# Fills in one shared score bank, VectorE tiles in the third banks, an earlier last output product, and Q ahead of K in an attention-and-gated-MLP kernel

## The chip, the cores and the metric

One core of a Trainium2 chip. The metric is the device time of one execution in microseconds (us). All runs used here are of the fast state; most executions of a kernel agree within half a per cent (61 of the 64 of the kernel before are within 0.5% of their common median). "Span" is the time from the first to the last instruction of the profiled execution; it is about 2 us shorter than the device time of the same execution (736.1 of 737.96 for the kernel before). The experiments ran in three later calls, on three chips. The kernel before ran in each of them, with medians of 739.65, 739.92 and 738.97 us, so kernels of different calls are compared by their ratios to before rather than by their medians.

## The reference

```python
x: (1, 2048, 512) bf16                  # 2048 tokens
q, k, v = (x @ wqkv) -> 32 heads of 16
o = softmax(q @ k.T / 4) @ v            # 32 x 2048 x 2048 scores
a = o @ wo
b = ((x @ w_gate) * (x @ w_up)) @ w_down    # inner width 1376
g = sigmoid((x * gate_w).sum(-1))
out = g * a + (1 - g) * b
```

## The kernel before

The exponential is the big item: the 32 x 2048 x 2048 scores are 2048 tiles of 128 keys (partitions) by 512 queries. A tile goes one of two ways. **ScalarE tiles** (1536 at first) take a table exponential, two or three tiles in one instruction. **VectorE tiles** (512 at first) take an integer trick on VectorE plus three shifted copies, shared by VectorE and GpSimd. TensorE makes scores, the products with V, and all "fills": the Q, K, V, gate, up, down and output products.

The kernel divides PSUM into eight banks of 128 x 512 fp32: slots A and B of three banks each (`psS`, 128 x 3072), one bank X (`psX`) and one for the sums over V (`psO`). ScalarE reads the first two or three banks of the slots in turn. Five more words: a **cell** is a place in SBUF for one tile of exponentials (in `PT`, or in `wv`, `hT` or `wd` while these are not needed for their own data); it is free again when its product with V is done. A **quad** is four heads, a **head block** eight, a **chunk** 512 queries. A **pack** is four 32-wide matmuls that run side by side (in the trace of before the four start within about 0.01 us of each other, and packs of 512 columns that follow each other directly 0.215 to 0.228 us apart). The normalised output of a quad goes to `OT`, for every second quad by way of `OX` and four DMAs.

The kernel is a **planner**: while it is built, it plays the five engines forward with assumed durations and fixes each engine's instruction order. Each engine then runs in that order and waits on semaphores. `st["ua"]` counts ScalarE tiles issued so far; every fill has a position `pos` in that count.

```python
# a score group: which third bank goes to what (cut)
use3 = "a"                                   # three ScalarE tiles
if late > (FA1 if b else FA0): use3 = "f"    # a late fill takes the third bank
elif lag >= (LA1 if b else LA0): use3 = "d"  # a VectorE tile takes it
if dleft and lag > LC: convert()             # VectorE too far behind: give a tile to ScalarE
...
# where a fill may start (cut)
if st["ua"] < 96 or late > FA1: cand.append(slots[1][2])
if st["ua"] < 96 or late > FA0: cand.append(slots[0][2])
if st["ua"] < 96 or not can or late > XF or not d_pick(...): cand.append(X)
...
FA0 = 20; FA1 = 0; LA0 = 2; LA1 = 0; XF = 24; LC = 3
```

The tail of before: when all scores are done, four banks take the output product of the last chunk over all but the last quad (`tail_first`, 16 packs); then the last quad is normalised in four pieces, its packs are added, and four combines (`ost`, two buffers) go out by DMA.

## Time and profile before

| | before |
|---|---|
| device time, median | 739.64 us (740.08 with the run beside the changed kernel) |
| profiled span | 736.1 us |
| ScalarE busy | 709.0 us, 96% |
| TensorE busy | 695.5 us, 94% |
| first exponential / end of the last | 10.1 / 723.4 us |

The profile's first part gives each engine's busy time, then the span in 40 slices with the busy share in tenths, then the chain that ended last. A row of groups reads: line, engine, operation, output<-input with shapes, count | busy us, mean ns | idle before, and what ended it. The lines themselves are shown in the prediction. I split the time with the start of each exponential in the trace: time to the first; **floor** = 0.904 us for each two-tile instruction, 1.331 for each three-tile one, the durations from start to start when nothing is in the way, and 0.478 for a single tile (worked out from these two; no kernel has more than two); **stalls** = the rest up to the end of the last exponential; **tail**.

### The profile page before, as it was taken

The numbers are of one execution on the slowest core, as the hardware profiler recorded it, in microseconds if no ns is written. First come the engines' busy times: TensorE is split into PE (matmuls) and PEld (weight loads), VectorE is DVE, ScalarE is ACT, GpSimd is POOL, SyncE is SP. The second block draws the span as 40 slices with busy tenths as digits, with TensorE's granted clock in tenths as the row PEclk, the third lists the DMA queues.
The fourth block names the chain that finished last, engine by engine and source line by source line (L and its number), as shares of the span: only waits on it lengthen the run. The fifth ranks groups of instructions, "written<-read, shape, count | busy, mean of one in ns | idle before, by whom it ended". The sixth has DMA issues, their size and how long they took to land.

```text
span 736.1 us, 21656 instructions
## 1 busy us (share of the span) xinstructions
PE 695.5 (94%) x9177; PEld 204.7 (28%) x9177; DVE 636.2 (86%) x1179; ACT 709.0 (96%) x703; POOL 409.6 (56%) x432
## 2 busy tenths in 40 slices
PE   8999999999999999999989999999999899899897
PEld 3323333322222222222222222222222222222222
DVE  5888978798898999989979988889889789998785
ACT  5999999899999999999999999999999899999994
POOL 3756885154656556566775654466566454655341
PEclk9999999999999999999999999999999999999999
DMA  7700000002000010000000100000000100000000
GB/s 143 243 4 17 20 17 18 17 4 97 18 19 19 13 32 24 20 17 17 20 8 21 38 27 17 17 12 12 20 17 19 32 18 20 16 21 17 17 19 31
DMA packets 31015, 21.66 MB, mean 29 GB/s; under 512 B 18344, under 2 KB 25928, under 8 KB 30920
## 3 DMA queue, kind: packets, MB, share of 16 engines
q1 hardware_dynamic: 29048, 19.49, 8.9%
q8 instruction: 73, 1.20, 0.7%
q10 hardware_dynamic: 1872, 0.79, 0.5%
q14 instruction: 22, 0.18, 0.1%
HBM read 15.11 MB, written 2.35 MB: 24 GB/s over the span
## 4 chain that ended last, share of the span: by engine, by line
ACT 64%; PE 8%; DVE 1%; DMA 1%; issue 0%; SPq 0%; POOL 0%; DVEq 0%
ACT PT L1545 52%; ACT wv L1545 13%; PE psO L1081 3%; PE psS L502 2%; PE psS L900 1%; PE psX L900 1%; PE psS L1092 1%; DVE PT L958 1%; DVE PT L1014 0%; DMA OT<-OX 0%; SPq L1166 0%; DMA out_dram<-ost 0%; DVE ost L793 0%; POOL OX L1153 0%; DVE usb L701 0%
## 5 line engine op out<-in xcount | busy, mean ns | idle before, releaser
L1545 ACT ACTIVATE PT<-psS 128x1024 bf16<-128x1024 f32 (+1 forms) x509 | 556.7, 1278 | 6.8 <-PE psO L1081 4.4
L1017 POOL TENSOR_SCALAR PT<-PT 128x1024 int16<-128x1024 int16 x325 | 336.3, 1046 | 259.7 <-DVE PT L1014 153.7
L900 PE MATMUL psS<-QM,KE 32*128 32x512 bf16 x1731 | 270.2, 385 | 10.6 <-ACT PT L1545 5.0
L958 DVE TENSOR_SCALAR PT<-psX 128x512 int16<-128x512 f32 x313 | 214.3, 685 | 42.3 <-PE psS L900 36.1
L1081 PE MATMUL psO<-PT,VS 128*18 128x512 bf16 x1656 | 222.2, 381 | 1.0 <-POOL PT L1017 0.4
L1081 PE MATMUL psO<-PT,VD 128*18 128x512 bf16 x1428 | 210.2, 382 | 1.9 <-POOL PT L1017 1.2
L1014 DVE TENSOR_SCALAR PT<-PT 128x1024 int16<-128x1024 int16 x382 | 169.4, 481 | 4.6 <-PE psO L1081 1.7
L1545 ACT ACTIVATE wv<-psS 128x1024 bf16<-128x1024 f32 (+1 forms) x122 | 142.1, 1204 | 0.3
L900 PE MATMUL psX<-QM,KE 32*128 32x512 bf16 x317 | 120.4, 380 | 15.0 <-ACT PT L1545 5.5
L958 DVE TENSOR_SCALAR PT<-psS 128x512 int16<-128x512 f32 x183 | 123.8, 684 | 12.2 <-PE psS L900 10.9
L900 PEld LDWEIGHTS psS<-QM,KE 32*128 32x128 bf16 x1731 | 68.5, 91 | 165.3 <-ACT PT L1545 67.5
L900 PEld LDWEIGHTS psX<-QM,KE 32*128 32x128 bf16 x317 | 28.7, 90 | 144.1 <-issue 44.5
L1081 PE MATMUL psO<-wv,VS 128*18 128x512 bf16 x256 | 65.4, 382 | 0.6 <-POOL PT L1017 0.3
L1081 PEld LDWEIGHTS psO<-PT,VS 128*18 128x18 bf16 x1656 | 52.1, 88 | 44.1 <-issue 29.9
L1081 PEld LDWEIGHTS psO<-PT,VD 128*18 128x18 bf16 x1428 | 49.2, 88 | 44.2 <-issue 24.9
L502 PE MATMUL psS<-wd,hT 128*32 128x512 bf16 (+1 forms) x704 | 53.2, 384 | 1.0 <-ACT PT L1545 0.9
L502 PE MATMUL psS<-xT,wu 128*32 128x512 bf16 x656 | 53.4, 384 | 0.4 <-DVE QM L557 0.2
L502 PE MATMUL psS<-xT,wg 128*32 128x512 bf16 x640 | 49.4, 383 | 0.2 <-DVE usb L701 0.2
L1545 ACT ACTIVATE hT<-psS 128x1024 bf16<-128x1024 f32 (+1 forms) x39 | 40.5, 1114 | 6.1 <-PE psS L900 6.0
L701 DVE CAST usb<-psS 128x512 bf16<-128x512 f32 (+1 forms) x42 | 28.6, 681 | 4.5 <-PE psS L502 4.3
L733 DVE TENSOR_TENSOR hT<-psS,usb 128x512 bf16<-128x512 f32 (+1 forms) x41 | 27.9, 681 | 2.9 <-PE psS L502 2.2
L1153 POOL TENSOR_TENSOR OX<-oraw,rb 128x512 bf16<-128x512 f32 x15 | 19.1, 1273 | 12.9 <-DVE PT L1014 7.9
(97 smaller groups left out, 471.1 us busy)
## 6 DMA issues: line engine op xcount, KB each, us to landing
rb<-rscr SPq DMA_DIRECT2D x31, 256.0 KB
out_dram<-ost SPq DMA_DIRECT2D x16, 128.0 KB, 1.7
wu<-in_B_w_up_dram SPq DMA_DIRECT2D x1, 1376.0 KB, 10.2
wg<-in_B_w_gate_dram SPq DMA_DIRECT2D x1, 1376.0 KB, 12.7
wd<-in_B_w_down_dram SPq DMA_DIRECT2D x1, 1280.0 KB, 6.1
OT<-OX SPq DMA_DIRECT2D x60, 16.0 KB, 1.8
wo<-in_A_wo_dram SPq DMA_DIRECT2D x1, 512.0 KB, 10.6
den<-oraw SPq DMA_DIRECT2D x31, 8.0 KB
```

What stands on the lines that cost most here:

```text
L502: return e.matmul(out_ap[32 * q : 32 * q + w, :], lhs[:, 32 * q : 32 * q + w], rhs, start=s0, stop=s1, tile_position=(0, 32 * q), skip_gro ...
L701: lambda v: v.tensor_copy(usb[0:w, n % 2, :], bk.ap[0:w, :]),
L733: lambda v: v.tensor_tensor(hT[0:w, f, :], bk.ap[0:w, :], usb[0:w, n % 2, :], ALU.mult),
L900: r = e.matmul(bk.ap, KE[32 * j : 32 * j + 32, b, kt * 128 : (kt + 1) * 128], QM[32 * j : 32 * j + 32, p, b, :], start=True, stop=True, ti ...
L958: lambda v: v.tensor_scalar(cell_ap(pr["cell"] + i, 1, mybir.dt.int16), bk.ap, CB, 0.0, ALU.add, ALU.max),
L1014: fn = lambda v: v.tensor_single_scalar(cell_ap(c, n, I16), cell_ap(pr["cell"], n, I16), 32.0 * k, ALU.add)
L1017: fn = lambda g: g.tensor_scalar(cell_ap(c, n, I16), cell_ap(pr["cell"], n, I16), 32.0 * k, 1.0, ALU.add, ALU.mult)
L1081: r = e.matmul(psO[32 * j : 32 * j + VW, :], pv_stationary(m, kt, j, k), cell_ap(cell, 1), start=s0, stop=s1, tile_position=(0, 32 * j), s ...
L1092: r = e.matmul(DB.ap[32 * j : 32 * j + 32, :], ones[:, k, :], cell_ap(cell, 1), start=s0, stop=s1, tile_position=(0, 32 * j), skip_group_c ...
L1153: lambda e: e.tensor_tensor(dst, oraw[:, s, :], rb[:, s, :], ALU.mult),
L1545: lambda a: a.activation(cell_ap(c, n), src, ACT.Exp, scale=LN2 / 128.0),
```

## The change

The intent is to keep fills out of the slots, so that score groups do not wait for a fill's eviction; to drive ScalarE with the measured overhead; and to take work from both ends.

```diff
-        FA0 = 20          # fills may take third banks when late
-        FA1 = 0
-        LA0 = 2
-        LA1 = 0
-        XF = 24
+        FA0 = 99          # practically never
+        FA1 = 99
+        LA0 = 0           # VectorE tiles take third banks readily
+        LA1 = 1
+        XF = -99          # X is always open to fills
-        LC = 3            # conversion limit
+        LC = 6
-        LAP = 0.0
+        LAP = 0.1
-                0.065 + 0.4267 * n,     # assumed exponential time, n tiles
+                0.052 + 0.4267 * n,
-                        lat=2.2,        # OT<-OX transfer
+                        lat=3.2,
-        ED = 330
+        ED = 380
-        F0 = 190.0; WP = 40.0; F1 = 1500.0
+        F0 = 210.0; WP = 36.0; WL = 18.0; F1 = 1490.0
... (start)
-        for f, bk in ((f_k(0, 0, 0), slots[0][2]), (f_q(0, 0, 0), slots[1][2])):
+        for f, bk in ((f_q(0, 0, 0), slots[1][2]), (f_k(0, 0, 0), slots[0][2])):
+                if b == ch == 0:        # first K evicted by ScalarE
+                    ev_k[b, ch] = add("act", [last], lambda a: a.activation(dst, bk.ap, ACT.Copy), ...)
-            if can and t + PACK > max(tE, tL) + 0.08:
+            if ua == 0 or (can and t + PACK > max(tE, tL) + 0.08):   # no fill before the first scores
... (tail)
-            for tt in range(4 if c < NCH - 1 else 0):
-                fills.append(f_wo(c, tt, ...))
+            for tt in range(4):        # the last chunk's product too, as fills at NA - WL
+                fills.append(f_wo(c, tt, ... if c < NCH - 1 else NA - WL))
-        def tail_first(t, force=False): ...    (removed)
+        # combine() of these writes fp32 partial sums, o_dst = part[:, tt, :];
+        # the final combine adds the last quad to them, into four buffers wk[:, tt, :]
```

(Cut: the same assumed time in two more places, two bookkeeping lines, the loop's end condition.)

More of the change, by code (lines that the diff above doesn't have):

```diff
@@ L527, in evac @@
                 bk.need += 1
+                dst = KE[:, b, ch * 512 : (ch + 1) * 512]
+                if b == ch == 0:
+                    ev_k[b, ch] = add(
+                        "act", [last], lambda a: a.activation(dst, bk.ap, ACT.Copy), 0.48, lat=0.66, cb=lambda k: bk.readers.append(k)
+                    )
+                    return
                 ev_k[b, ch] = add(
@@ L530, in evac @@
                     [last],
-                    lambda v: v.tensor_copy(KE[:, b, ch * 512 : (ch + 1) * 512], bk.ap),
+                    lambda v: v.tensor_copy(dst, bk.ap),
                     0.61,
@@ L786, in _build @@
         otfree = {}
+        ev_part = {}
+        part = xT[:, :, 512:1536].bitcast(F32)
         def combine(t, bank_ap, last, cb=None, halves=None):
             c, tt = divmod(t, 4)
+            fin = t >= T - 4 and halves is None
+            o_dst = ost[:, t % 2, :] if t < T - 4 else part[:, tt, :] if not fin else wk[:, tt, :]
+            src = part[:, tt, :] if fin else b_ap(t)
             k = add(
                 "dve",
-                [last, ev_b[c, tt], ogate["g"], o_out.get(t - 2)],
-                lambda v: v.scalar_tensor_tensor(
-                    ost[:, t % 2, :], bank_ap, gval[:, t : t + 1], b_ap(t), ALU.mult, ALU.add
-                ),
+                [last, ev_b[c, tt], ogate["g"]] + ([o_out.get(t - 2)] if t < T - 4 else [ev_part[tt]] if fin else [pe["last"]]),
+                lambda v: v.scalar_tensor_tensor(o_dst, bank_ap, gval[:, t : t + 1], src, ALU.mult, ALU.add),
                 0.67,
@@ L799, in combine @@
             )
+            if t >= T - 4 and not fin:
+                ev_part[tt] = k
+                return
             bfree[t] = k
@@ L803, in combine @@
                 [k],
-                lambda e: e.dma_start(out2[t * 128 : (t + 1) * 128, :], ost[:, t % 2, :]),
+                lambda e: e.dma_start(out2[t * 128 : (t + 1) * 128, :], o_dst),
                 0.1,
@@ L812, in f_wo @@
             t = 4 * c + tt
+            lastc = c == NCH - 1
             packs = [
                 (
-                    lambda bk, b=b: col(bk.ap, OT[:, (NB * c + b) % NOT, tt * 128 : (tt + 1) * 128], wo[:, b, :], b == 0, b == NB - 1),
+                    lambda bk, b=b: col(
+                        bk.ap,
+                        OT[:, (NB * c + b) % NOT, tt * 128 : (tt + 1) * 128],
+                        woz[:, 0, :] if lastc and b == NB - 1 else wo[:, b, :],
+                        b == 0,
+                        b == NB - 1,
+                    ),
                     PACK,
@@ L825, in evac @@
                 bk.need += 1
-                combine(t, bk.ap, last, cb=lambda k: bk.readers.append(k))
+                combine(t, bk.ap, last, cb=lambda k: bk.readers.append(k), halves=True if lastc else None)
             def deps():
+                if lastc:
+                    if any(f.name[0] in "ugkvq" for f in fills):
+                        return [None]
+                    return [d_wo, d_woz[0], ev_b.get((c, tt)), o_mult.get(NM - 2)] + [o_ot.get(NB * c + b) for b in range(NB - 1)]
                 if t >= 2 and t - 2 not in o_out:
@@ L1194, in _build @@
         GP = 200.0
-        F0 = 190.0
-        WP = 40.0
-        F1 = 1500.0
+        F0 = 210.0
+        WP = 36.0
+        WL = 18.0
+        F1 = 1490.0
         fills.append(f_gate(GP))
@@ L1212, in _build @@
                 fills.append({"u": f_u, "g": f_g, "d": f_d}[kind](c, i, pos))
-            for tt in range(4 if c < NCH - 1 else 0):
-                fills.append(f_wo(c, tt, max(PER * NQ * (c + 1) + WP, f0 + step * (c + 1) + 4.0) + 9.0 * tt))
+            for tt in range(4):
+                fills.append(f_wo(c, tt, max(PER * NQ * (c + 1) + WP, f0 + step * (c + 1) + 4.0) + 9.0 * tt if c < NCH - 1 else NA - WL))
         for c in range(NCH - 1):
@@ L1270, in do_fill @@
                 f.bank.need -= 1
-                FE.append((f, f.bank, f.t0, k))
                 f.evac(f.bank, k)
+                FE.append((f, f.bank, f.t0, k, qs["dve"][-1] if qs["dve"] else None))
                 if f.name[0] == "v":
@@ L1281, in act_need @@
             for a in exps:
-                tt += 0.065 + 0.4267 * len(a[0])
+                tt += 0.052 + 0.4267 * len(a[0])
             return tt
@@ L1436, in pe_step @@
                     return True
-            if can and t + PACK > max(tE, tL) + 0.08:
+            if ua == 0 or (can and t + PACK > max(tE, tL) + 0.08):
                 return False
-            if not aleft and not dleft and (pv_ready(t) is None) and tail_first(t):
-                return True
             if dleft and lag_() > LDO:
@@ L1457, in _build @@
         tailb = []
-        def tail_first(t, force=False):
-            c = NCH - 1
-            tt = len(tailb)
-            if tt == 4:
-                return False
-            deps = [d_wo, d_woz[0]] + [o_ot.get(NB * c + b) for b in range(NB - 1)] + [o_mult.get(NM - 2)]
-            for bk in (X, slots[1][2], slots[1][0], slots[0][0], slots[1][1], slots[0][1]):
-                if bk in tailb or bk.free_at() is None or not (force or bank_free(bk, t)):
-                    continue
-                if not force and any(d is None or d.end is None or d.end + SEM > t for d in deps):
-                    return False
-                deps += bk.take(99)
-                tailb.append(bk)
-                cs = slice(tt * 128, (tt + 1) * 128)
-                def fn(e):
-                    r = None
-                    for b in range(NB):
-                        r = col(bk.ap, OT[:, (NB * c + b) % NOT, cs], wo[:, b, :] if b < NB - 1 else woz[:, 0, :], b == 0, False)(e)
-                    return r
-                pe_run(deps, fn, 4 * PACK, "c", t)
-                return True
-            return False
         def filler(t, can=True):
@@ L1545, in act_step @@
                 lambda a: a.activation(cell_ap(c, n), src, ACT.Exp, scale=LN2 / 128.0),
-                0.065 + 0.4267 * n,
-                lat=0.065 + 0.4267 * n + 0.21,
+                0.052 + 0.4267 * n,
+                lat=0.052 + 0.4267 * n + 0.21,
             )
@@ L1666, in _build @@
         o_xt[0] = o_xt[-KD]
-        for f, bk in ((f_k(0, 0, 0), slots[0][2]), (f_q(0, 0, 0), slots[1][2])):
+        for f, bk in ((f_q(0, 0, 0), slots[1][2]), (f_k(0, 0, 0), slots[0][2])):
             fills.append(f)
             start_fill(f, bk)
-            if f.name == "k00":
-                f.deps = lambda: [d_wk[0]]
+            if f.name == "q00":
+                f.deps = lambda: [d_wq[0]]
                 f.pdeps = [[o_xt[-1 - kt]] for kt in range(KD)]
@@ L1681, in _build @@
                 clock[e] += 0.02
-            if pvst["m"] >= NM:
+            if pvst["m"] >= NM and not fills and st["fill"] is None:
                 break
@@ L1696, in _build @@
         assert not fills and st["fill"] is None, [f.name for f in fills]
-        while len(tailb) < 4:
-            assert tail_first(clock["pe"], True)
         c = NCH - 1
+        tailb = [X, slots[1][2], slots[1][0], slots[0][0]]
         lastpv = pvst["last"]
@@ L1726, in _build @@
                 pe_run(
-                    [mt],
-                    col(tailb[tt].ap, OX[:, (NB - 1) % 2, cs], woz[:, 1, :], False, True),
+                    [mt] + tailb[tt].take(99),
+                    col(tailb[tt].ap, OX[:, (NB - 1) % 2, cs], woz[:, 1, :], True, True),
                     PACK,
```

## The prediction

> **What bounds the kernel now.** I read the busy table and the 40 slices first, to see which engine is full and when.
>
> ```profile
> PE 695.5 (94%) x9177; PEld 204.7 (28%) x9177; DVE 636.2 (86%) x1179; ACT 709.0 (96%) x703; POOL 409.6 (56%) x432
> ...
> ACT  5999999899999999999999999999999899999994
> ...
> ACT 64%; PE 8%; DVE 1%; DMA 1%; issue 0%; SPq 0%; POOL 0%; DVEq 0%
> ```
>
> ScalarE is full in every slice but the first and last, and the chain that ended last lies on it for 64% of the span. TensorE is close behind. So time can come from four places only: what ACT does before its first exponential, the length of its exponentials, its stalls between them, and what follows the last one. For the second I read ACT's groups with shapes kept apart.
>
> ```profile
> L1545 ACT ACTIVATE PT<-psS 128x1024 bf16<-128x1024 f32 x367 | 379.9, 1158 | 1.2 <-PE psO L1081 0.7 <-PE psS L900 0.4
> L1545 ACT ACTIVATE PT<-psS 128x1536 bf16<-128x1536 f32 x142 | 225.1, 1590 | 5.6 <-PE psO L1081 3.7 <-PE psS L900 1.9
> L1545 ACT ACTIVATE wv<-psS 128x1024 bf16<-128x1024 f32 x110 | 122.8, 1161 | 0.3
> ```
>
> With the groups that write hT, wd and wv there are 530 instructions of two score tiles (367+110+36+17) and 162 of three (142+12+5+3): 530x2 + 162x3 = 1546 tiles. The plan starts with 1536 ScalarE tiles and 512 VectorE tiles, so 10 tiles were "converted" to ScalarE because VectorE lagged. The means above include overlap with the next instruction. From start to start in the timeline, back to back, the two-tile form takes 0.904 us and the three-tile form 1.331: 0.427 per tile and 0.05 per instruction. Unstalled, the stream needs 530x0.904 + 162x1.331 = 694.7 us. It begins at 10.1 and ends at 723.4, so it lasts 713.3: **18.6 us are stalls**. The waits view shows only part of them, because short ones hide inside the records.
>
> ```profile
> ACT PT L1545 <- PE psO L1081: 4.4, 4, 3.3
> ...
> ACT PT L1545 <- PE psS L900: 2.3, 3, 1.0
> ```
>
> Taking starts one by one, 3.7 us are lost at 134.5 and 2.3 at 572 to 577; thirteen stalls over 0.3 us, these included, make 10.8 and the rest, 7.8, is crumbs. In the timeline the one at 134.5 is a run of K and Q products for the last head block on TensorE from 134.3 to 136.9 with no probability-times-V product, so no cell came free for ScalarE (its releaser is psO). The one at 572 is TensorE, in order, waiting 1.3 us for an OT<-OX transfer before an output product; a drop of the TensorE clock to half for 3.4 us follows.
>
> The end is read from the timeline of VectorE:
>
> ```profile
> 729.86 0.75 DVE L793 SCALAR_TENSOR_TENSOR ost<-psX,gval,wq 128x512 bf16<-128x512 f32 x1 [1.71 <-PE psX L502]
> 730.53 0.28 DVE L1722 TENSOR_TENSOR OX<-psO,rb 128x128 bf16<-128x128 f32 x1
> 730.73 0.74 DVE L793 SCALAR_TENSOR_TENSOR ost<-psS,gval,wq 128x512 bf16<-128x512 f32 x1
> 732.44 1.58 DVE L793 SCALAR_TENSOR_TENSOR ost<-psS,gval,wq 128x512 bf16<-128x512 f32 x2 [0.97 <-DMA out_dram<-ost]
> ```
>
> After the last exponential: products with V until 726.1, sixteen packs of the output product 726.0 to 729.4, the last packs, four combines of 0.75 us, with 0.97 us waited for the two-deep output buffer to drain. The tail is 736.1 - 723.4 = 12.7 us.
>
> [...] So the choice of two or three tiles is nearly free: three tiles cost 0.025 us less in one three-tile instruction than in one and a half two-tile ones. [...] moving the first K eviction to ScalarE should add no table load; the trace shows one load of 1.28 us. [...] every fill takes a bank away from scores; the trace has both kinds writing psS and psX. [...] here the output transfers, from SyncE, take a median 1.7.
>
> **The change, part by part.**
>
> *Fills in X, VectorE scores in third banks.* Nothing is removed from the work. Today fills sit mostly in third banks (640 to 656 of the up, gate and down matmuls each write psS, under 50 psX), and 317 of 502 VectorE tiles come from X. After, a fill past the start takes X only; X is free for VectorE between fills. Grouping: with two ScalarE tiles and one VectorE tile (A groups), or three ScalarE tiles (B groups), the 3:1 ratio of the tiles asks A = 3B, so 2048/3 = 683 groups against 692 now: 512 of two tiles and 171 of three. That is the same mix as now, about 0.5 us of ScalarE saved. If all were two-tile: 768 instructions, 76x0.05 = 3.8 us more. The gain must be in stalls: a score group no longer waits for the eviction of a fill in its slot.
>
> *Conversion limit 3 to 6.* Each conversion costs ScalarE 0.427 us. I take two of the ten to remain: 8x0.427 = **-3.4 us**. VectorE gets 8 tiles back, each 0.61 plus its share of copies (412 copies of pairs for 502 tiles, 0.35 us each: 0.29), some 7 us over the whole run, and it has 14% idle.
>
> *Timing constants, places of fills.* ACT's assumed overhead goes from 0.065 to 0.052, which is what the trace shows; the OT transfer from 2.2 to 3.2 us, where the timeline has 4.3 from the first of four issues to landing; gate/up work starts later (190 to 210) and wd's cells serve as tiles longer (330 to 380), which relieves the crowding behind the 134.5 stall. I take about a third of the stalls off: 18.6 to 12, **-6.6 us**.
>
> *First Q ahead of first K.* The trace has K's product 5.78 to 6.83, Q's from 6.70, when wq landed, two Q evictions to 9.21, a V product from 8.68 squeezed in front, first scores at 9.67, first exponential at 10.11. After: Q cannot start before wq lands, 6.70; K follows at 7.56 (four packs of 0.214), ends near 8.6; ScalarE evicts it by 9.3 while VectorE does Q's masks; the new rule lets no fill in before the first scores: 9.4, exponential near 9.8. **-0.3 us.** Q first is no gain by itself; the parallel eviction and the rule are.
>
> *Last output product early.* It removes twelve of sixteen packs' worth of wait from the tail, and the four-deep result buffer removes the 0.97 us. If all were early, the end would be PV end 726.1 + 1.1 for Ln, Exp, multiply, then four combines and a transfer, near 733.3, or -2.8. But the partial product needs the normalised output of the last but one quad, which GpSimd finished at 722.36, 1.1 us before the last exponential, and the four fills may only use X, one after the other: 1.05 (product) + 0.75 (combine) + 0.15 = 1.95 us each. They end near 730.2, and the last combines stand behind them in VectorE's order: end near 736. I take **-0.7 us** between the two.
>
> Sum: -0.5 -3.4 -6.6 -0.3 -0.7 = -11.5, so a span near 724.6. The median run stands 739.64 - 736.1 = 3.5 above the profiled span: **728.1 us**, -1.6%.
>
> **Rivals.** (1) X becomes the bottleneck. 169 fills (16 each of Q, K, V and output, 88 up and gate, 16 down, one gate) in 713 us leave 4.2 us each, against about 2 for a fill that runs undisturbed; in the stretch 96 to 290, where Q, K and V of new heads crowd, it is 3.5. A late K starves ScalarE as at 134.5; two or three such stalls give 735 to 742. Against: fills over 99 tiles late may use third banks again. (2) TensorE is the real bound: it idles only 6%, and more two-tile groups, each with two mode changes of 0.1 us, would fill it. Then nothing is gained: 738 to 740. Against: group counts stay near 683. (3) VectorE in third banks delays ScalarE directly: a tile's eviction (0.68 us) must end within one turn of the slot, about 2 us, or the group goes short. Then stalls stay: 733. (4) The plan fits the chip better than I grant and nearly all stalls over 0.3 us go, with the tail's -2.8: -10.8 -3.4 -2.8 -0.8 gives 722, past 2%.
>
> **Range and chances.** Rival 4 is as likely as 1 and 2 together; the constants were set from measured durations, which speaks for gain. 80% range 720 to 738. Faster by over 2% means under 724.9: 0.27. Within 2%: 0.69. Slower by over 2% needs a lasting queue on X: 0.04.
>
> **What would show it.** Fills of up, gate and down writing psX, VectorE tiles mostly from psS; ScalarE tiles near 1538 and instructions near 690; no single ACT wait over 2 us; first exponential near 9.8; no wait on out_dram<-ost; last exponential to end between 10 and 13 us. I am wrong if the conversions do not fall, if the instructions rise toward 768, if K or Q products run late and ACT waits on psS, or if the partial products push the last combines out.

## The result

The changed kernel takes **731.62 us** (median of 4, 729.51 to 732.69), before 740.08. The ratio is 0.9877, 95% interval 0.9837 to 0.9917. Here and below a ratio is the mean time of one kernel's fast runs over that of the other's of the same rounds, so it is not quite the ratio of the medians quoted. The time lies in the predicted range, 3.5 us above the predicted value.

The busy table, the slices and the chain of the changed kernel's page:

```profile
PE 696.8 (96%) x9207; PEld 204.2 (28%) x9207; DVE 635.9 (87%) x1196; ACT 704.4 (97%) x687; POOL 419.9 (58%) x443
...
ACT  4999999999999999999999999999999999999993
...
PEclk9999997999999999999999999999999999999999
...
ACT 85%; PE 12%; DVE 1%; DMA 1%; issue 0%; ACTq 0%; DVEq 0%
```

ScalarE still bounds the kernel, now for 85% of the last chain. Something new stands in the clock row, `PEclk`: the seventh slice has 7 tenths of the TensorE clock. ScalarE's groups by shape and its waits, in the changed kernel:

```profile
L1541 ACT ACTIVATE PT<-psS 128x1024 bf16<-128x1024 f32 x321 | 348.0, 1228 | 0.6 <-PE psS L923 0.4 <-PE psO L1104 0.2
L1541 ACT ACTIVATE PT<-psS 128x1536 bf16<-128x1536 f32 x152 | 250.9, 1657 | 0.3 <-PE psS L923 0.3
```

```profile
ACT hT L1541 <- PE psS L923: 2.5, 4, 1.0
ACT wv L1541 <- PE psS L923: 1.6, 3, 0.9
ACT PT L1541 <- PE psS L923: 0.7, 3, 0.3
ACT wd L1541 <- PE psS L923: 0.6, 2, 0.5
ACT PT L1541 <- PE psO L1104: 0.2, 1, 0.2
```

Waits for psO, a cell freed by a product with V, were 4.4 us and are 0.2. The longest single wait between exponentials is 1.0 us, where it was 3.3. The VectorE groups show where its tiles and the evictions of fills are: before, with the fills in psS, then changed, with the fills in psX:

```profile
L958 DVE TENSOR_SCALAR PT<-psX 128x512 int16<-128x512 f32 x313 | 214.3, 685 | 42.3 <-PE psS L900 36.1
...
L958 DVE TENSOR_SCALAR PT<-psS 128x512 int16<-128x512 f32 x183 | 123.8, 684 | 12.2 <-PE psS L900 10.9
...
L701 DVE CAST usb<-psS 128x512 bf16<-128x512 f32 (+1 forms) x42 | 28.6, 681 | 4.5 <-PE psS L502 4.3
```

```profile
L981 DVE TENSOR_SCALAR PT<-psS 128x512 int16<-128x512 f32 x429 | 290.9, 685 | 41.5 <-PE psS L923 36.4 <-PE psO L1104 1.7
...
L981 DVE TENSOR_SCALAR PT<-psX 128x512 int16<-128x512 f32 x77 | 53.0, 688 | 17.1 <-PE psS L923 16.6
L707 DVE CAST usb<-psX 128x512 bf16<-128x512 f32 (+1 forms) x44 | 30.0, 682 | 2.3 <-PE psX L502 1.8
```

The split of the time, for these two and for the runs that follow (from the starts in each profiled execution; "in half clock" are the stalls after exponentials that start within 1 us of a stretch in which the TensorE clock is granted at half):

| kernel | first exp. | tiles / instr. | floor | stalls (in half clock) | tail | span | median, ratio to before |
|---|---|---|---|---|---|---|---|
| before | 10.1 | 1546 / 692 | 694.7 | 18.6 (1.2) | 12.7 | 736.1 | 740.08 |
| changed | 10.7 | 1536 / 675 | 689.6 | 15.8 (4.4) | 13.0 | 729.1 | 731.62, 0.9877 |
| a_third | 10.3 | 1536 / 721 | 691.9 | 25.3 (2.2) | 15.5 | 743.0 | 746.02, 1.0097 |
| b_fillX | 9.9 | 1540 / 670 | 691.1 | 16.7 (1.6) | 12.3 | 730.0 | 732.87, 0.9903 |
| b_seed5 | 10.1 | 1548 / 690 | 695.5 | 22.0 (7.2) | 13.3 | 740.9 | 743.54, 1.0046 |
| b_fillX_seed5 | 10.1 | 1539 / 683 | 691.3 | 16.2 (1.3) | 13.1 | 730.7 | 732.88, 0.9912 |
| a_seed5 | 12.0 | 1536 / 680 | 689.9 | 23.3 (5.6) | 15.0 | 740.2 | 740.83, 1.0003 |
| a_seed5_k185 | 12.2 | 1536 / 679 | 689.8 | 15.6 (5.3) | 16.4 | 733.9 | 735.95, 0.9948 |
| a_wqload | 9.4 | 1536 / 675 | 689.6 | 14.5 (2.8) | 13.0 | 726.5 | 730.07, 0.9861 |
| a_oldtail | 12.4 | 1536 / 674 | 689.6 | 15.7 (4.4) | 12.6 | 730.2 | 730.60, 0.9872 |
| a_gate32 | 9.5 | 1536 / 675 | 689.6 | 15.5 (4.0) | 13.0 | 727.6 | 729.48, 0.9849 |
| a_gp330 | 9.0 | 1536 / 678 | 689.8 | 12.9 (2.0) | 14.2 | 725.9 | 727.78, 0.9836 |
| a_gate1 | 11.8 | 1536 / 675 | 689.6 | 14.2 (2.5) | 13.0 | 728.5 | 728.40, 0.9858 |
| best1 | 10.6 | 1536 / 673 | 689.5 | 12.0 (1.3) | 13.0 | 725.1 | 727.06, 0.9838 |

From before to changed: floor -5.1, stalls -2.8, start +0.6, tail +0.3 make -7.0, the difference of the spans. Each row is one profiled execution, and the start varies from one execution to the next (see a_wqload), so the rows are best compared in floor and stalls. Names that begin with a_ stem from the changed kernel, with b_ from the kernel before.

### The profile page after: what moved, and what is told of

Read it like the earlier page. It is cut to its first block, busy times and chain, and to the rows that moved or that the text cites. A ratio compares the mean times of both kernels' runs of the same rounds, so it can differ in the third digit from the quotient of the medians.

```text
span 729.1 us, 21770 instructions
## 1 busy us (share of the span) xinstructions
PE 696.8 (96%) x9207; PEld 204.2 (28%) x9207; DVE 635.9 (87%) x1196; ACT 704.4 (97%) x687; POOL 419.9 (58%) x443
## 4 chain that ended last, share of the span: by engine, by line
ACT 85%; PE 12%; DVE 1%; DMA 1%; issue 0%; ACTq 0%; DVEq 0%
ACT PT L1541 61%; ACT wv L1541 15%; ACT wd L1541 5%; ACT hT L1541 4%; PE psO L1104 3%; PE psS L923 3%; PE psX L502 3%; DMA wq<-in_A_wqkv_dram 1%; PE psS L502 1%; PE psS L586 0%; DVE PT L981 0%; PE psX L586 0%; PE psX L923 0%; DVE wk L804 0%; PE psS L1115 0%
## 5 line engine op out<-in xcount | busy, mean ns | idle before, releaser
L981 DVE TENSOR_SCALAR PT<-psS 128x512 int16<-128x512 f32 x429 | 290.9, 685 | 41.5 <-PE psS L923 36.4
L981 DVE TENSOR_SCALAR PT<-psX 128x512 int16<-128x512 f32 x77 | 53.0, 688 | 17.1 <-PE psS L923 16.6
L502 PE MATMUL psX<-wd,hT 128*32 128x512 bf16 (+1 forms) x704 | 55.7, 384 | 0.0
L502 PE MATMUL psX<-xT,wu 128*32 128x512 bf16 x688 | 55.5, 388 | 0.2 <-DVE QM L563 0.2
L502 PE MATMUL psX<-xT,wg 128*32 128x512 bf16 x688 | 53.8, 384 | 0.3 <-DVE usb L707 0.3
L1541 ACT ACTIVATE wd<-psS 128x1024 bf16<-128x1024 f32 (+1 forms) x39 | 45.8, 1248 | 0.6 <-PE psS L923 0.6
L1040 POOL TENSOR_SCALAR wd<-PT 128x1024 int16<-128x1024 int16 x27 | 28.0, 1044 | 8.8 <-PE psO L1104 3.4
L923 PE MATMUL psX<-QM,KE 32*128 32x512 bf16 x80 | 30.4, 380 | 2.6 <-ACT KE L531 0.8
L707 DVE CAST usb<-psX 128x512 bf16<-128x512 f32 (+1 forms) x44 | 30.0, 682 | 2.3 <-PE psX L502 1.8
L739 DVE TENSOR_TENSOR hT<-psX,usb 128x512 bf16<-128x512 f32 (+1 forms) x44 | 30.0, 681 | 2.1 <-PE psX L502 1.8
## 6 DMA issues: line engine op xcount, KB each, us to landing
wg<-in_B_w_gate_dram SPq DMA_DIRECT2D x1, 1376.0 KB, 12.2
wo<-in_A_wo_dram SPq DMA_DIRECT2D x1, 512.0 KB, 12.6
```

Source lines behind the costliest of these rows:

```text
L502: return e.matmul(out_ap[32 * q : 32 * q + w, :], lhs[:, 32 * q : 32 * q + w], rhs, start=s0, stop=s1, tile_position=(0, 32 * q), skip_gro ...
L707: lambda v: v.tensor_copy(usb[0:w, n % 2, :], bk.ap[0:w, :]),
L739: lambda v: v.tensor_tensor(hT[0:w, f, :], bk.ap[0:w, :], usb[0:w, n % 2, :], ALU.mult),
L923: r = e.matmul(bk.ap, KE[32 * j : 32 * j + 32, b, kt * 128 : (kt + 1) * 128], QM[32 * j : 32 * j + 32, p, b, :], start=True, stop=True, ti ...
L981: lambda v: v.tensor_scalar(cell_ap(pr["cell"] + i, 1, mybir.dt.int16), bk.ap, CB, 0.0, ALU.add, ALU.max),
L1040: fn = lambda g: g.tensor_scalar(cell_ap(c, n, I16), cell_ap(pr["cell"], n, I16), 32.0 * k, 1.0, ALU.add, ALU.mult)
```

## The experiments

Three theories stood at first. **Theory 1:** the fill rule makes the gain. **Theory 2:** the timing constants, moved positions and the early tail do. **Theory 3:** the gain is a fortunate order of fills, found for one seed of the jitter that spreads their positions. Runs of one call share the runs of before.

### a_third: the changed kernel without the fill rule

```diff
-        FA0 = 99; FA1 = 99; LA0 = 0; LA1 = 1; XF = -99
+        FA0 = 20; FA1 = 0; LA0 = 2; LA1 = 0; XF = 24
```

> The changed kernel with the fill rule undone (fills may take third banks again, X not preferred). Theory 1 (the rule is the source of the gain: no conversions, fewer short groups, fewer stalls): the gain of 1.2% is lost or nearly so, ratio to before 0.995 to 1.01, more ScalarE instructions than 675 (about 700 to 730), stalls of the exponential stream over 20 us. Theory 2 (timing constants, moved positions and the early tail make the gain): ratio stays 0.98 to 0.99.

746.02 us, ratio 1.0097 (1.0068 to 1.0125): not only is the gain gone, the rest of the change alone is slower than before. ScalarE needs 721 instructions, stalls are 25.3 us. Its groups by shape (compare the 152 three-tile ones above):

```profile
L1541 ACT ACTIVATE PT<-psS 128x1024 bf16<-128x1024 f32 x467 | 467.6, 1165 | 5.6 <-PE psO L1104 4.4 <-PE psS L923 1.1
L1541 ACT ACTIVATE PT<-psS 128x1536 bf16<-128x1536 f32 x84 | 135.4, 1612 | 0.0
```

A fill that holds a third bank leaves two tiles to the instruction, and the waits for psO are back at 4.4 us. Theory 2 falls.

### b_fillX: the fill rule alone, on the kernel before

The reverse of the diff above, on the kernel before.

> The kernel before with the fill rule alone (five numbers). Theory 1: conversions fall from 10 to 4 or less, ScalarE instructions to some 670, and most of the gain is there, ratio 0.988 to 0.994. Theory 2: no gain alone, ratio 0.997 to 1.003.

732.87 us, ratio 0.9903 (0.9868 to 0.9938): nearly the whole gain, with LC still 3. Conversions fell from 10 to 4 (1540 tiles), instructions from 692 to 670. ScalarE's largest groups (before has 367 of two tiles and 142 of three there):

```profile
L1545 ACT ACTIVATE PT<-psS 128x1024 bf16<-128x1024 f32 x286 | 305.8, 1178 | 0.1
L1545 ACT ACTIVATE PT<-psS 128x1536 bf16<-128x1536 f32 x165 | 264.3, 1612 | 0.5 <-PE psS L900 0.5
```

Of the 6.1 us that the span lost, 3.6 are floor and 1.9 stalls: ScalarE mainly has less to do, and waits less besides. The five numbers are most of the change. Everything else together is worth 1.3 us by the medians and 1.9 by the two ratios, whose intervals overlap.

**Conversions** need no run. The changed kernel built with LC = 3 is the same program as with 6: in the plan VectorE never falls behind by more than 3. So the limit did nothing. The fill rule alone takes away six of the ten conversions (b_fillX, with LC still 3); the last four go only with the rest of the change, and what in it takes them was not tested.

### a_seed5 and b_seed5: another order of the fills

```diff
-        SEED = 2
+        SEED = 5
```

> The changed kernel with another seed of the small jitter that spreads the fills' positions (2 to 5); every rule stays. It is the control for luck. Theory 1: the rules make the gain, so the ratio to before stays 0.985 to 0.992. Theory 3 (the positions were picked for this one seed and any other order loses much of it): slower than the changed kernel by 5 to 9 us, ratio to before 0.995 to 1.002, with the loss in stalls, not in instruction counts.

> The kernel before with seed 5 in place of 2 for the jitter of the fills' positions. Under the changed rules seed 5 cost 10 us (a_seed5). If the old rules are as sensitive, the time moves by 4 to 10 us up (744 to 750); if positions matter only under the changed rules, where one bank serves the fills in turn, it stays within 2.5 us of before (737 to 742).

With seed 5 the changed kernel takes 740.83 us, ratio 1.0003 (0.9985 to 1.0021). The gain is gone, in stalls (23.3 us) and tail (15.0), not in counts, as theory 3 had it. The late start of its profile, 12.0 us, is not the seed's doing: up to 42 us all engines have the same instructions in the same order as in the changed kernel, and in this execution the TensorE clock was at half from 7.8 to 11.2 us. The kernel before loses too, but less: 743.54, ratio 1.0046 (1.0028 to 1.0063), between the two expectations. In a_seed5 ScalarE waits 1.9 us at 163.8 and 2.9 at 172.7. The timelines of ScalarE and, for the second wait, of TensorE (score and fill products only) there:

```profile
163.79 1.45 ACT L1541 ACTIVATE wv<-psS 128x1536 bf16<-128x1536 f32 x1 [1.89 <-PE psS L923]
...
172.65 1.02 ACT L1541 ACTIVATE wv<-psS 128x1024 bf16<-128x1024 f32 x1 [2.89 <-PE psS L923]
```

```profile
168.51 1.04 PE L502 MATMUL psX<-xT,wg 128*32 128x512 bf16 x16
170.35 1.05 PE L502 MATMUL psX<-xT,wk 128*32 128x512 bf16 x16 [0.58 <-DVE hT L739]
172.20 0.39 PE L923 MATMUL psX<-QM,KE 32*128 32x512 bf16 x1 [0.80 <-DVE KE L537]
```

The K product at 170.35 waited 0.58 us until the gate product before it had left X (the multiply into hT), and the scores at 172.20 waited 0.80 for K's eviction: a late K behind another fill in the one bank, the prediction's first rival.

### a_seed5_k185: is it the late K?

```diff
 # on top of a_seed5
-            (200.0, 280.0, [("q", 3, 0)] + [("k", 3, ch) for ch in range(4)]),
+            (185.0, 265.0, [("q", 3, 0)] + [("k", 3, ch) for ch in range(4)]),
```

> The seed-5 kernel with one change: the last head block's Q and K products are due 15 tiles earlier (185 to 265 instead of 200 to 280). In a_seed5 the three stalls at 153.5, 160.9 and 168.7 us (7.0 us together) were scores waiting for a K product that stood behind other fills in X. Theory L (late K in the one bank is what other positions cost): those stalls go, the stalls between 150 and 200 us fall from 7.2 to under 1.5, and the time falls by 5 to 9 us against a_seed5 (740.8), to 732 to 736. Theory P (any order but the picked one is bad for many small reasons): stalls appear elsewhere and the time stays within 3 us of a_seed5.

The stalls between 150 and 200 us went from 7.2 to 0.8 us, all stalls from 23.3 to 15.6, the level of the changed kernel. The time fell 4.9 us to 735.95, just short of the 5 expected (by the ratios, which span two calls, 4.1). The tail of this order is 1.4 us longer, and the clock of the profiled execution was at half again at the start. So the late K is shown to bring all of the extra stalls and about half of what seed 5 costs (9.2 us by the medians); its tail, 16.4 us against 13.0, is the larger part of what remains.

### b_fillX_seed5: does the rule itself hang on the seed?

> The kernel before with the fill rule alone and seed 5. It completes two by two: before 739.7 (seed 2) and 743.5 (seed 5); fill rule alone 732.9 (seed 2). If the rule's gain does not hang on the seed, 736 to 738 here; if the rule only pays with the picked order, 741 to 745.

732.88 us, 3 us better than the better of the two expectations. With the rule alone both seeds take 732.9. So **the rule's gain is not the luck of one order**, as far as two orders can tell (0.990 and 0.991 of before, whose seed-5 form stands at 1.005). What hangs on the seed is the rest of the change: with seed 5 it costs 8 us on top of the rule. Which of the other constants makes it so sensitive is open: gate and up work that starts at 210, the exponential planned at 0.052 instead of 0.065, and the others were not taken apart.

### a_wqload: the start

```diff
-        d_wk[0] = load("act", wk[:, :, 0:128], ...)
         d_wq[0] = load("act", wq[:, :, 0:128], ...)
+        d_wk[0] = load("act", wk[:, :, 0:128], ...)
```

> The changed kernel with the first wq load issued before the first wk load; nothing else moves (the same instructions in the same order on every compute engine). In the changed kernel Q waits for wq until 7.52 and the first exponential comes at 10.66. If Q's place ahead of K costs because wq is loaded second, Q starts near 6.0 to 6.7 and the first exponential near 9.4 to 9.9, so the time falls by 0.8 to 1.2 us (0.1 to 0.2%), at the edge of what 3 rounds show. If the wait is that of the DMA queues in general, wk is then late instead and the first exponential stays at 10.5 or later.

730.07 us, first exponential at 9.38. The ratio, 0.9861 (0.9827 to 0.9896), cannot be told from the changed kernel's, but the timelines can. TensorE in the changed kernel, then in a_wqload:

```profile
7.52 1.05 PE L502 MATMUL psS<-xT,wq 128*32 128x512 bf16 x16 [1.70 <-DMA wq<-in_A_wqkv_dram]
8.38 1.05 PE L502 MATMUL psS<-xT,wk 128*32 128x512 bf16 x16
10.22 0.37 PE L923 MATMUL psX<-QM,KE 32*128 32x512 bf16 x1 [0.79 <-ACT KE L531]
```

```profile
6.23 1.05 PE L502 MATMUL psS<-xT,wq 128*32 128x512 bf16 x16 [0.77 <-DMA wq<-in_A_wqkv_dram]
7.09 1.05 PE L502 MATMUL psS<-xT,wk 128*32 128x512 bf16 x16
8.93 0.37 PE L923 MATMUL psX<-QM,KE 32*128 32x512 bf16 x1 [0.79 <-ACT KE L531]
```

The product of Q was put first but its weights were left second. Over all traces, with wk loaded first, the first scores came at 9.5 to 9.7 us in the old order of products (four traces) and at 9.8 to 11.9 in the new (five). With wq first they came at 8.6 to 9.0 in three, and at 10.1 and 11.3 in best1 and a_gate1, where the second load, now wk, landed only at 8.3. In best1, K's product waited for it. In a_gate1 it hid behind Q's product, which took 1.90 us instead of 1.05, as K's did: full clock was granted only from 10.4 us. So the second load of the pair is what the scores wait for where the clock is full, and putting Q's weights second costs Q's place in front; but a landing varies by over 1 us from run to run (the second 128 KB load, issued 0.5 us after the first, landed 0.8 to 2.0 us after it over these traces), and in the three latest starts of the five with wk first the TensorE clock was at half besides.

### a_oldtail: the tail of before on the changed kernel

`tail_first` and the two-deep `ost` are put back, the last chunk's fills are taken out of the list after the jitter, so that the order up to the last 30 us stays.

> The changed kernel with the tail of before: no product of the last chunk ahead of the end, all in the tail, two-deep output buffer; everything else as changed, and the same order up to the last 30 us. My theory (the early products go into TensorE's full last stretch and delay the last products with V by as much as they save): from the last exponential to the end 12.5 to 13.5 us as in the changed kernel (13.0), time within 1.5 us of it. Rival (the early tail is worth what the diff intends): the tail grows to 15 us or more and the time by 2 to 3 us.

730.60 us, ratio 0.9872 (0.9848 to 0.9897) against 0.9877; tail 12.6 us against 13.0. The early product is worth nothing. VectorE and ScalarE of a_oldtail, then of the changed kernel:

```profile
720.24 0.28 ACT L1722 ACTIVATE oraw<-psS 128x128 f32<-128x128 f32 x1 [2.65 <-PE psS L1098]
```

```profile
726.49 1.58 DVE L799 SCALAR_TENSOR_TENSOR ost<-psS,gval,wq 128x512 bf16<-128x512 f32 x2 [0.96 <-DMA out_dram<-ost]
```

```profile
721.76 0.28 ACT L1710 ACTIVATE oraw<-psS 128x128 f32<-128x128 f32 x1 [5.63 <-PE psS L1115]
```

```profile
722.62 0.75 DVE L804 SCALAR_TENSOR_TENSOR xT<-psX,gval,wq 128x512 f32<-128x512 f32 x1 [1.41 <-PE psX L502]
723.29 0.68 DVE L1717 TENSOR_TENSOR OX<-psO,rb 128x128 bf16<-128x128 f32 x3
724.08 0.75 DVE L804 SCALAR_TENSOR_TENSOR wk<-psX,gval,xT 128x512 bf16<-128x512 f32 x1
724.94 2.06 DVE L804 SCALAR_TENSOR_TENSOR wk<-psS,gval,xT 128x512 bf16<-128x512 f32 x3
```

The wait for the output DMA (0.96 us) is gone, but ScalarE's normalisation now waits 5.6 us instead of 2.7 for the last products with V: the sixteen packs (3.4 us) moved from behind them to between them. The fourth partial combine, at 722.62, also stands ahead of the first multiply of the last quad, whose factor was ready at 722.4.

### a_gate32, a_gp330, a_gate1: the half-clock stretch

In the changed kernel the TensorE clock is at half from 107.8 to 118.0 us, and again for 3.4 us from 483.2. Windows of the changed kernel, then of the kernel before (start and end, length, busy us of PE, PEld, DVE, ACT, POOL with counts, granted clock, DMA share, GB/s):

```profile
107.50:118.00 10.50, 9.92 (x95) 2.62 (x93) 6.51 (x12) 8.95 (x9) 6.16 (x6) 0.51 0.02 3
```

```profile
107.50:118.00 10.50, 9.42 (x133) 3.62 (x130) 9.22 (x18) 10.50 (x11) 6.29 (x7) 1.00 0.02 3
```

TensorE looks as busy but does 95 matmuls instead of 133, and ScalarE loses 1.55 us in the records alone. Both kernels run the gate's product there (64 matmuls of one column), from 104.3 and 104.6 us. Three edits on a_wqload: four 32-wide column tiles in place of one 128-wide (a_gate32); `GP = 330.0` for 200 (a_gp330); only one of the four slices, 16 matmuls, which gives a wrong result on purpose (a_gate1, relative error 0.025).

> As a_wqload, with the gate's product in four column tiles of 32 instead of full 128-wide stationaries: the same result, the same order of everything else. In five of six traces so far the TensorE clock falls to half 2 to 5 us after the gate product starts (10.2 us long in the changed kernel and in a_wqload). Theory A (the full-width weight loads of the gate bring the drop): no half-clock stretch near 105 to 118, ScalarE stalls between 100 and 150 fall from 3.0 to under 1.2, time 1.5 to 2.5 us below a_wqload. Theory B (the drop comes of the dense work before it, whatever the gate is): the stretch stays at 105 to 118 and the time is that of a_wqload within 1 us.

> As a_wqload, with the gate's product due at tile 330 instead of 200, some 60 us later; the order of fills around it changes too. Theory A: the half-clock stretch moves with it to about 165 to 180. Theory B: it stays near 107 to 117. Time within 3 us of a_wqload either way, as the order around it changes.

> As a_wqload, with only the first of the four 128-row slices in each gate product: 16 matmuls instead of 64, the result wrong on purpose, all else in the same order. The half-clock stretch moved with the gate in a_gp330 (175.4 with the gate at 173.4). Theory A2 (the gate's run of one-column products brings the drop): no half-clock stretch at 105 to 118, stalls between 100 and 150 us under 1.2 instead of 3.0, time 1.5 to 2.5 us under a_wqload (727.6 to 728.6). Theory B2 (something due at the same place, such as what the gate delays): the stretch stays.

The windows 105 to 120 of a_gate32 and a_gate1, and 170 to 185 of a_gp330:

```profile
105.00:120.00 15.00, 14.26 (x287) 4.46 (x291) 11.19 (x23) 13.65 (x14) 8.21 (x9) 0.66 0.02 4
```

```profile
105.00:120.00 15.00, 12.77 (x108) 3.29 (x104) 11.39 (x24) 13.49 (x14) 8.08 (x9) 0.66 0.02 3
```

```profile
170.00:185.00 15.00, 13.14 (x153) 4.61 (x153) 11.12 (x23) 14.38 (x15) 7.48 (x7) 0.68 0.07 22
```

The stretch follows the gate (a_gp330: gate from 173.4, stretch from 175.4), but neither narrower weights nor a quarter of the matmuls removes it: theories A and A2 both fall in the form I wrote them. What fits these three runs is the opposite: not the gate's load but the **lack of load**. The stretches in these traces are 3.4, 6.8, 10.2, 13.7 and 17.1 us long, multiples of 3.41 (the one at 574.2 in the kernel before is 3.41 long, those at 107.8 and 483.2 in the changed kernel 10.24 and 3.41), so I took 3.41 us as the window. Busy time does not show a lack: from 104.0 to 107.5 in the changed kernel TensorE is busy for 2.59 of the 3.5 us. As a measure I took the columns that TensorE streams in 3.41 us as a share of what it could (512 columns in 0.2135 us, the plan's figure for a pack, where the traces show packs 0.215 us apart; four concurrent 32-wide matmuls counted once). The median over the changed kernel's trace is 0.75. In the window before the stretch at 107.8 it is 0.19; in the kernel before it never falls under 0.38 between 102 and 122, and the clock holds (granted 1.00). It was 0.19 there in the window that ends at 572.8, while TensorE waited 1.30 us for the OT transfer, and the only stretch inside that trace starts at 574.2. In the ten traces that I took it from, the windows before the inner stretches hold 0.13 to 0.50. It is no sharp rule: a window of 0.31, at 381.0 in the kernel before, passed without a stretch, while one of 0.38 came before that of a_gp330. On this reading one-column products and waits for banks leave the array too little to stream, and fewer of them (a_gate1) need not help; that matmuls of one column count for little is a guess, which no run isolates. This is a correlation: no run kept the array streaming through the gate's product, so it is not shown by experiment, and these runs do not settle what share lets the clock fall.

How much time goes with the clock can be read from the 64 executions of the kernel before in the three calls. At a mean granted clock of 0.996 they took 737.2 to 738.9 us, at 0.987 to 0.989 they took 742.9 to 744.3; a line through all 64 gives 5.8 us for each 0.01. That is most of the spread between executions of one kernel, and b_seed5, at a mean of 0.982 over its 19 runs, would by this line lose more than it did. It is again a correlation: it does not tell whether waits lower the clock or the lower clock lengthens the waits.

The time: a_gate32 729.48 (0.9849), a_gate1 728.40 (0.9858), a_gp330 727.78 (0.9836, 0.9812 to 0.9859). The last has fewer stalls outside the stretch as well, so its gain is that of another order as much as of the gate.

### best1: a version that beats both

```diff
 # on top of a_wqload
-            (200.0, 280.0, [("q", 3, 0)] + ...          # last head block's Q, K
+            (185.0, 265.0, [("q", 3, 0)] + ...
-        GP = 200.0; F0 = 210.0; WP = 36.0; SEED = 2
+        GP = 400.0; F0 = 230.0; WP = 42.0; SEED = 1
```

The settings were picked by letting the kernel's own planner try some hundreds.

> The version to beat both: the changed kernel with wq loaded first, the last head block's Q and K 15 tiles earlier, the gate at 400, gate/up work from 230, seed 1. Expected: first exponential near 9.3, 1536 tiles, stalls 12 to 13, tail 13: 725 to 728, ratio to before 0.980 to 0.984, and so another seed than 2 does as well when the Q and K products are early.

**727.06 us**, ratio 0.9838 (0.9816 to 0.9861), correct, with a seed other than 2; only the first exponential was later (10.6) than expected. It is a picked order, so it does not show that any seed does as well once Q and K are early, as the expectation has it; a_seed5_k185 speaks against that. Its waits:

```profile
ACT hT L1541 <- PE psS L923: 2.5, 4, 1.0
...
ACT wv L1541 <- PE psS L923: 0.4, 1, 0.4
ACT PT L1541 <- PE psS L923: 0.2, 1, 0.2
```

Of its 12.0 us of stalls 8.3 are crumbs under 0.3 us each; 2.6 lie before 50 us. What remains to win is small without changing the work itself.

## Why the prediction was right or wrong, point by point

- **The bound: right. The source of the gain: right in part.** ScalarE bounds both kernels; the time came from floor (5.1 of 7.0 us) and stalls (2.8). The fill rule was named as the place of the gain, and a_third and b_fillX show it. But the sum put the gain elsewhere: -6.6 under the constants and positions, -3.4 under the conversion limit, and only -0.5 under the rule. The constants and positions without the rule (a_third) have 25.3 us of stalls, 6.7 more than before.
- **Grouping: right.** 675 instructions against the predicted 683 to 690, hence -0.85 us by the 0.05 us of each, where -0.5 was in the sum.
- **"Conversion limit 3 to 6": right size, wrong cause.** All ten conversions went (-4.3 us, predicted -3.4), but the limit is never reached; six of them went by the fill rule alone.
- **Stalls, "a third of the stalls off, -6.6": mis-sized, and the largest miss of the sum.** They fell 2.8 us. Outside half-clock stretches they went from 17.4 to 11.4 us, -6.0, near the step. Inside, they rose from 1.2 to 4.4. (The wait for the OT transfer that ran into the stretch at 574 counts as outside here; counted as inside, the fall outside is 4.6.) I had seen the half-clock stretch at 574 us in the trace of before and did not ask what would bring more of them.
- **Start, "-0.3": wrong.** It was +0.6. I reckoned with wq landing at 6.7, as in the trace of before; it landed at 7.4. The step used one trace's landing for a transfer that varied by over a microsecond, and the second load of the pair bears that on the path. With wq first the step's 9.8 was met in three of five traces (9.0 to 9.5) and missed in two (10.6 and 11.8). That the move adds no table load was right: the first K's eviction took ScalarE 0.60 us and there is one table load in the trace (1.28 us), as before.
- **Tail, "-0.7": what was seen was right, one cost was left out.** It was +0.3. The prediction saw the wait for the last but one quad, the single bank X and the place of the last combines in VectorE's order. It left out that the packs themselves push the last products with V back by 2.9 us.
- **The rivals.** X as bottleneck (the first) is real but not for the picked order: it cost a_seed5 about half of its gain. TensorE as the bound (the second) did not come: the groups became fewer. VectorE in third banks delaying ScalarE (the third) shows no wait that names it: TensorE's waits for a bank that an exponential on VectorE held were 3.9 us before, and the view of waits of the changed kernel lists none.

The sum was -11.5 us of span; -7.0 came, the difference being stalls +3.8, tail +1.0 and start +0.9, less 1.2 more won on the floor (the parts are rounded). So the span was missed by 4.5 us and the median by 3.5 only because the step from span to median, taken as 3.5, was 2.5 this time: that part was luck.

Two readings of the prediction were off without weight in the sum. Of the down matmuls all 704 wrote psS, not 640 to 656. And the fills behind the stall at 134.5 were not of K and Q alone: there was no product with V from 131.3 to 136.9 us, and the MLP's gate products stand among the fills.

## What to carry to other kernels

When two kinds of work share buffers, give the work that is off the critical path a buffer of its own, and let it queue there; here that alone was worth nearly the whole gain, in both orders of the queue that were tried. The price is that a short-deadline item can stand behind a long one, so its due time must come earlier. Change a kernel's random seed or the like once before you credit a change: it tells what a rule gives from what a picked order gives. And when work is moved off the end of a kernel, look whether the engine it moves to is idle there.
